# Reading the moving operand of a matmul as pairs of columns from its two halves

## The chip, the core and the metric

The kernel runs on one core of one Trainium2 chip. The metric is the device time of one launch in microseconds (us). The kernel before took 1817.81 us, the median of three runs (1817.16 to 1818.10).

## The reference

```python
x = A_x                                              # 1 x 2048 x 1024, float32
g = _sigmoid((x * gate_w).sum(-1, keepdims=True))
# A: Fourier mixing as dense matrices
a = jnp.einsum("bsd,ed->bse", x, dft_hid_re)
b = jnp.einsum("bsd,ed->bse", x, dft_hid_im)
y = jnp.einsum("ts,bse->bte", dft_seq_re, a) - jnp.einsum("ts,bse->bte", dft_seq_im, b)
# B: feed-forward, F = 3584
h = jnp.einsum("bsd,df->bsf", x, w1) + b1
r = jnp.where(h > 0, h, 0)
out = jnp.einsum("bsf,fd->bsd", r * r, w2) + b2
return g * y + (1 - g) * out
```

## The kernel before

**Stages.** Four matrix products follow one another. X multiplies `x` with the two hidden-dimension matrices (`w4`) and keeps the result `ab` in HBM. C multiplies the sequence matrices (`ct`) with `ab` and applies the gate. H multiplies `w1` with `x`, adds the bias, applies relu and square, and keeps `h` in HBM. O multiplies `w2` with `h`, adds the bias, applies `1 - g`, and adds C's part. By the loads of their inputs in the trace, C begins at about 241 us, H at about 810, O at about 1279.

**Fewer products, more sums.** Each stage is split into two by two blocks, and seven products replace eight (`FACTORS`); most of these are split into seven again (`twice`). VectorE makes the sums of blocks that this needs (tiles `sum`, `raw`, and the sums on results: `ab`, `y`, `h`, `o`, `u`).

**Three matmuls for one.** Every block is a tile of 128 partitions by 2 by 512 elements. An `Operand` splits it: ScalarE writes `hi`, the block rounded to the matmul's float32 type fp32r, and VectorE writes `lo`, what the rounding took away. `Group.run` (L542) then issues for each row block `r`, each half `kk` of the tile and each of the three pairs (hi·hi, hi·lo, lo·hi) one matmul. In all of them the stationary operand `st` is 128 columns wide, the moving operand `mv` is 512 columns wide, and the result fills 128 by 512 in PSUM (tile `ps`). These are the wide matmuls. The only others are 44 matmuls of 128 columns in bf16 on a tile `ones`, at the start (`WARM`).

**Who sets the order.** Nothing runs as it is written. The functions record operations; `plan` (L1372) then goes through a model of the machine and hands out each engine's order, the order of the DMA queues, and which of 55 SBUF slots each tile gets, by due times counted back from the matmuls. The model's time for one wide matmul is the constant `MM` (L39), in microseconds; all due times scale with it. TensorE's own order is not planned: matmuls go as recorded. `emit` (L1524) writes everything out, so nearly every row of the profile has its line, L1542. SyncE issues most loads, GpSimd the stores, the loads that add into SBUF or HBM, and some loads that the plan puts there.

**Layouts.** `kernel` (L1559) lays the inputs out in numpy before the launch: `x4`, `w4`, `ct` and `w1a`/`w1b`/`w2` as tiles for the stages, `xn` for the gate; it turns the output back after it. Those steps are outside the device time.

Of the kernel before, what the change touches and what calls it, by code (L numbers as in the profile page):

```python
# [15 lines left out]
P = 128  # L16
S, D, F = 2048, 1024, 3584
# [18 lines left out]
MADE = {"T1": 2568, "T3": 11876}  # L36
TWICE_H = (1, 2, 5, 3, 4, 6, 7), (1, 2, 5, 3, 4, 6)

MM, MM_END, FIRST_MM = 0.2267, 0.18, 6.2  # L39
VEC, VEC_END, ACT, ACT_END = (0.07, 1.0417e-3), 0.39, (0.09, 0.843e-3, 0.04, 0.095), 0.41  # L40
ADDING = 0.85, 2.1, 2.2
ISSUE, RING, RATE, SEM, LANES = {"sync": 0.36, "scalar": 0.36, "gpsimd": 0.56}, {"sync": (1.8, 1.8), "scalar": (1.8, 1.8), "gpsimd": (1.6, 1.6)}, (420e3, 395e3), 0.06, 8
# [33 lines left out]
def gated_mix_kernel(ctx: ExitStack, tc: tile.TileContext, x4, xn, w4, ct, w1a, w1b, w2, b1, b2, gw, out):  # L76
# [143 lines left out]
    def run(*parts):  # L220

        for _ in zip_longest(*parts):
            pass
# [57 lines left out]
    class Part(Near):  # L281
# [21 lines left out]
        def load(self, engines):  # L303
            if self.lands:
                self.slots = [take("raw", width=self.width)]
                a, b = (b.at if isinstance(b, Kept) else b for b in self.blocks)
                at = self.slots[0][:, :, 0:self.width]
                next(engines).dma_start(at, a)
                nc.gpsimd.dma_start(at, b, accum_op=ADD)
            else:  # L310
                run(self.load_parts(engines))
# [24 lines left out]
        def sum(self):  # L336
            run(self.make_parts())
# [59 lines left out]
    class Operand:  # L397
# [28 lines left out]
        def sum(self):  # L426
            run(self.sum_parts())
# [86 lines left out]
    class Group:  # L514
# [27 lines left out]
        def run(self, st, mv, by_part=False):  # L542
            if not self.ps:
                self.prepare()
            self.at += 1
            ends = self.at % self.k == 0
            mms = [(r, kk, n) for r in range(self.rows) for kk in range(2) for n in range(3)]
            if by_part:
                mms.sort(key=lambda e: (e[1], e[0] // 2, e[2], e[0]) if e[1] == 0 else (e[1], e[2], e[0]))
            for r, kk, n in mms:  # L550
                a, b = ((st.hi, mv.hi), (st.hi, mv.lo), (st.lo, mv.hi))[n]
                nc.tensor.matmul(self.ps[r // self.per][:, r % self.per, :], a[:, kk, r * P:(r + 1) * P],
                                 b[:, kk, :], start=self.at == 1 and kk + n == 0 and not self.onto,
                                 stop=ends and kk == 1 and n == 2,
                                 skip_group_check=bool(self.at > self.k or self.onto))
                if ends and self.per == 1 and kk == 1 and n == 2:
                    self.done[0][0](r // 2, self.ps[r], r % 2)
                elif ends and (r % 2 or r == self.rows - 1) and kk == 1 and n == 2:
                    self.done[self.at // self.k - 1][0](r // 2, self.ps[r // 2])
            if self.at == self.k * len(self.done):  # L560
                banks.extend(self.pools)
# [1031 lines left out]
```

## Time and profile before

| | |
|---|---|
| median of three runs | 1817.81 us |
| profiled execution, first to last instruction (its span) | 1816.2 us |
| outside the span, against the median | 1.6 us |
| TensorE busy | 1799.8 us, 99% |
| VectorE busy | 1711.6 us, 94% |
| ScalarE busy | 1157.5 us, 64% |
| GpSimd busy | 284.2 us, 16% |
| moved by DMA | 562.63 MB, 310 GB/s |
| mean granted TensorE clock | 0.999 |

The profile gives the span of its execution alone; the time outside it is taken from the runs. [...] And TensorE's weight load (PEld) lies beside the matmul before it.

### The profile page before, as it was taken

The page shows a single profiled execution, that of the slowest core. Times are in us where ns is not written, and L with a number is a line of the kernel's source. Part 1 is how long each engine was busy: PE and PEld are TensorE (multiplying, and loading weights), DVE is VectorE, ACT ScalarE, POOL GpSimd, SP SyncE. Part 2 cuts the span into 40 slices and gives each one's busy share as a digit, 9 for nine tenths or more (in the row PEclk, how much of TensorE's full clock was granted, in tenths as well). Part 3 has the DMA queues.
Part 4 walks back from the last instruction along what each step waited for, and adds up shares of the span by engine and source line. Part 5 has one row for each costly group of instructions (what it writes and reads, how often), then busy time and mean ns, then how long its engine had stood idle before and what let it go on. Part 6 is the DMA issues. An engine that isn't in the chain of part 4 may idle for free. (4 is left out here: it accounts for less than half of the span.)

```text
span 1816.2 us, 22349 instructions
## 1 busy us (share of the span) xinstructions
PE 1799.8 (99%) x7940; PEld 1484.5 (82%) x7940; DVE 1711.6 (94%) x1698; ACT 1157.5 (64%) x1274; POOL 284.2 (16%) x415
## 2 busy tenths in 40 slices
PE   9999999999999999999999999999999999999998
PEld 7888878888888888888878888788888888888886
DVE  8999989999999999999779999878998999999997
ACT  6465655774666664666583739967886567575662
POOL 1212112111211100111120201111121021101121
PEclk9999999999999999999999999999999999999999
DMA  9999999999998899989998889999999999979986
GB/s 376 322 393 380 384 331 302 323 273 292 261 354 264 227 306 383 311 216 351 314 371 278 279 299 329 375 381 327 345 362 253 335 241 303 328 192 349 316 218 149
DMA packets 158607, 562.63 MB, mean 310 GB/s; under 512 B 17808, under 2 KB 18080, under 8 KB 158496
## 3 DMA queue, kind: packets, MB, share of 16 engines
q1 hardware_dynamic: 98496, 351.99, 51.4%
q0 software_dynamic: 59712, 208.83, 43.1%
q8 instruction: 62, 1.02, 0.2%
q10 hardware_dynamic: 288, 0.39, 0.1%
q14 instruction: 49, 0.40, 0.1%
HBM read 402.28 MB, written 138.94 MB: 298 GB/s over the span
## 5 line engine op out<-in xcount | busy, mean ns | idle before, releaser
L1542 PE MATMUL ps<-hi 128*128 128x512 f32 x2188 | 852.2, 390 | 6.2 <-DVE h L1542 3.2
L1542 PE MATMUL ps<-hi,lo 128*128 128x512 f32 x2188 | 850.7, 389 | 1.0 <-DVE lo L1542 1.0
L1542 PE MATMUL ps<-lo,hi 128*128 128x512 f32 x2188 | 850.8, 389 | 0.6 <-DVE lo L1542 0.6
L1542 ACT ACTIVATE hi<-raw 128x1024 fp32r<-128x1024 f32 (+2 forms) x452 | 459.1, 1035 | 238.7 <-DVE raw L1542 76.1
L1542 PEld LDWEIGHTS ps<-hi 128*128 128x128 f32 x2188 | 410.6, 188 | 96.9 <-DVE h L1542 5.3
L1542 PEld LDWEIGHTS ps<-hi,lo 128*128 128x128 f32 x2188 | 410.7, 188 | 87.4 <-DVE lo L1542 1.8
L1542 PEld LDWEIGHTS ps<-lo,hi 128*128 128x128 f32 x2188 | 410.5, 188 | 86.4 <-DVE lo L1542 1.5
L1542 DVE TENSOR_TENSOR lo<-raw,hi 128x1024 fp32r<-128x1024 f32 (+2 forms) x385 | 451.5, 1190 | 29.1 <-ACT hi L1542 24.1
L1542 ACT ACTIVATE hi<-sum 128x1024 fp32r<-128x1024 f32 (+1 forms) x248 | 253.8, 1037 | 153.0 <-DVE sum L1542 103.3
L1542 DVE TENSOR_TENSOR lo<-sum,hi 128x1024 fp32r<-128x1024 f32 (+1 forms) x232 | 273.9, 1194 | 14.4 <-ACT hi L1542 5.4
L1542 PE MATMUL ps<-hi,both 128*128 128x512 f32 x888 | 285.0, 389 | 0.0
L1542 DVE TENSOR_TENSOR raw<-raw 128x1024 f32<-128x1024 f32 (+1 forms) x173 | 204.0, 1196 | 5.3 <-DMA raw<-in_w1a 2.6
L1542 PEld LDWEIGHTS ps<-hi,both 128*128 128x128 f32 x888 | 166.6, 188 | 34.7 <-DVE both L1542 0.2
L1542 DVE TENSOR_TENSOR sum<-raw 128x1024 f32<-128x1024 f32 (+2 forms) x180 | 175.6, 985 | 11.1 <-DMA raw<-in_w1a 2.3
L1542 PE MATMUL ps<-lo,both 128*128 128x512 f32 x444 | 172.7, 389 | 0.0
L1542 DVE TENSOR_TENSOR sum<-raw,sum 128x1024 f32<-128x1024 f32 (+2 forms) x135 | 141.3, 1049 | 2.3 <-DMA raw<-in_ct 1.4
L1542 ACT ACTIVATE u<-ps 128x1024 f32<-128x1024 f32 x104 | 101.2, 976 | 34.7 <-PE ps L1542 32.5
L1542 PEld LDWEIGHTS ps<-lo,both 128*128 128x128 f32 x444 | 83.4, 188 | 17.4
L1542 ACT ACTIVATE ps<-u 128x1024 f32<-128x1024 f32 x68 | 67.2, 989 | 35.5 <-DVE u L1542 16.3
L1542 DVE TENSOR_TENSOR u<-u,ps 128x1024 f32<-128x1024 f32 x74 | 86.8, 1184 | 1.9 <-PE ps L1542 1.0
L1542 ACT ACTIVATE both<-sum 128x512 fp32r<-128x512 f32 x74 | 46.3, 625 | 55.5 <-DVE sum L1542 49.2
L1542 DVE TENSOR_TENSOR h<-h,ps 128x1024 f32<-128x1024 f32 (+1 forms) x58 | 61.2, 1067 | 11.6 <-PE ps L1542 11.2
(82 smaller groups left out, 1002.2 us busy)
## 6 DMA issues: line engine op xcount, KB each, us to landing
raw<-in_ct SPq DMA_DIRECT2D x133, 512.0 KB, 8.9
raw<-h SPq DMA_DIRECT2D x104, 512.0 KB, 7.2
raw<-in_w SPq DMA_DIRECT2D x94, 512.0 KB, 9.0
raw<-copy SPq DMA_DIRECT2D x74, 512.0 KB, 7.1
raw<-ab SPq DMA_DIRECT2D x70, 512.0 KB, 10.0
raw<-in_x SPq DMA_DIRECT2D x51, 512.0 KB, 8.7
lo<-lo SPq DMA_DIRECT2D x50, 512.0 KB, 7.0
copy<-raw POOLq DMA_DIRECT2D x46, 512.0 KB, 9.3
```

What stands on the lines that cost most here:

```text
L1542: made = getattr(real[op.engine], op.name)(*(actual(a) for a in op.args), **{k: actual(v) for k, v in op.kwargs.items()})
```

## The change

One access pattern, one constant, and four layouts.

```diff
-MM, MM_END, FIRST_MM = 0.2267, 0.18, 6.2
+MM, MM_END, FIRST_MM = 0.2157, 0.18, 6.2
...
                 nc.tensor.matmul(self.ps[r // self.per][:, r % self.per, :], a[:, kk, r * P:(r + 1) * P],
-                                 b[:, kk, :], start=self.at == 1 and kk + n == 0 and not self.onto,
+                                 b[:, kk, :].rearrange("p (a b) -> p b a", a=2), start=self.at == 1 and kk + n == 0 and not self.onto,
...
+    seen = np.arange(512).reshape(2, 256).T.ravel()
+    twice = (512 * np.arange(4)[:, None] + seen[seen]).ravel()
...
-        "xn": x.reshape(P, 16, D).transpose(1, 0, 2),
-        "w4": np.stack([... for a in w]),
-        "ct": np.stack([... for a in c], axis=2),
+        "xn": x[twice].reshape(P, 16, D).transpose(1, 0, 2),
+        "w4": np.stack([... for a in w])[..., np.argsort(seen)],
+        "ct": np.stack([... for a in c], axis=2)[..., seen],
...
-    return np.ascontiguousarray(r.results[0]["out"].T).reshape(1, S, D)
+    return np.ascontiguousarray(r.results[0]["out"][:, np.argsort(twice)].T).reshape(1, S, D)
```

A wide matmul read the columns of its moving operand as 0, 1, 2, ... 511. Now it reads 0, 256, 1, 257, ... 255, 511: the pattern's inner dimension has two elements, 1024 bytes apart, and the outer one 256. The tile in SBUF, the stationary operand and the write to PSUM are as before. The columns of a result therefore stand in another order than those of its moving operand, and numpy's layouts make up for it: X's moving operand is stored the other way round, so `ab` is in plain order; H's result is in the order `seen`; O reads that in pairs again, so its columns are in `seen[seen]`, and `ct`, the gate's rows and the output follow. All of that is numpy's, before and after the launch; shapes and sizes of all transfers stay.

The constant changes the plan. Each engine still has the same instructions, by operation, names and shape, and the same number of DMAs on each queue; TensorE's row of matmuls is the same, and the orders of the four others change almost everywhere. Two places:

VectorE at the start of stage X, within its first twenty instructions; `sum` makes a sum of two blocks, `lo` a low part that a matmul waits for:

```order
-L1542 TENSOR_TENSOR lo<-sum,hi 128x1024
-L1542 TENSOR_TENSOR sum<-raw,sum 128x1024
-L1542 TENSOR_TENSOR lo<-raw,hi 128x1024
-L1542 TENSOR_TENSOR sum<-raw,sum 128x1024
-L1542 TENSOR_TENSOR lo<-sum,hi 128x1024
+L1542 TENSOR_TENSOR sum<-raw,sum 128x1024
+L1542 TENSOR_TENSOR lo<-sum,hi 128x1024
+L1542 TENSOR_TENSOR lo<-raw,hi 128x1024
+L1542 TENSOR_TENSOR lo<-sum,hi 128x1024
+L1542 TENSOR_TENSOR sum<-raw,sum 128x1024
```

One sum is made a place earlier and another a place later; the low parts between them keep their sequence.

ScalarE in the same stretch; `hi<-raw` and `hi<-sum` are the rounded parts of a block and of a sum, `u<-ps` empties a PSUM tile:

```order
 L1542 ACTIVATE hi<-raw 128x1024
 L1542 ACTIVATE u<-ps 128x1024
-L1542 ACTIVATE hi<-raw 128x1024
-L1542 ACTIVATE hi<-sum 128x1024
+L1542 ACTIVATE hi<-sum 128x1024
+L1542 ACTIVATE hi<-raw 128x1024
 L1542 ACTIVATE u<-ps 128x1024
 L1542 ACTIVATE hi<-sum 128x1024
```

Two rounded parts change places between two emptyings of PSUM.

More of the change, by code (lines that the diff above doesn't have):

```diff
@@ L1571 @@
              for j in range(2) for b in (16 + 6 * j,)]
+    seen = np.arange(512).reshape(2, 256).T.ravel()
+    twice = (512 * np.arange(4)[:, None] + seen[seen]).ravel()
     laid = {
         "x4": x.T.reshape(2, 2, 2, P, 4, 512).transpose(4, 0, 1, 3, 2, 5),
-        "xn": x.reshape(P, 16, D).transpose(1, 0, 2),
-        "w4": np.stack([a.T.reshape(2, 2, 2, P, 2, 512).transpose(4, 0, 1, 3, 2, 5) for a in w]),
-        "ct": np.stack([a.T.reshape(8, 2, P, 2, 2, 512).transpose(3, 4, 0, 2, 1, 5) for a in c], axis=2),
+        "xn": x[twice].reshape(P, 16, D).transpose(1, 0, 2),
+        "w4": np.stack([a.T.reshape(2, 2, 2, P, 2, 512).transpose(4, 0, 1, 3, 2, 5) for a in w])[..., np.argsort(seen)],
+        "ct": np.stack([a.T.reshape(8, 2, P, 2, 2, 512).transpose(3, 4, 0, 2, 1, 5) for a in c], axis=2)[..., seen],
         "w1a": w1[..., :2048].reshape(2, 2, 2, P, 2, 2, 512).transpose(4, 5, 0, 1, 3, 2, 6),
```

## The prediction

> **What bounds the kernel now.** I read the page's first part, then its chain and costliest groups, then the waits of TensorE, then the table by stage. The page's span and busy times, its chain, and the five groups of wide matmuls:
>
> ```profile
> span 1816.2 us, 22349 instructions
> PE 1799.8 (99%) x7940; PEld 1484.5 (82%) x7940; DVE 1711.6 (94%) x1698; ACT 1157.5 (64%) x1274; POOL 284.2 (16%) x415
> ...
> PE 27%; DVE 0%; issue 0%
> ...
> L1542 PE MATMUL ps<-hi 128*128 128x512 f32 x2188 | 852.2, 390 | 6.2 <-DVE h L1542 3.2
> L1542 PE MATMUL ps<-hi,lo 128*128 128x512 f32 x2188 | 850.7, 389 | 1.0 <-DVE lo L1542 1.0
> L1542 PE MATMUL ps<-lo,hi 128*128 128x512 f32 x2188 | 850.8, 389 | 0.6 <-DVE lo L1542 0.6
> ...
> L1542 PE MATMUL ps<-hi,both 128*128 128x512 f32 x888 | 285.0, 389 | 0.0
> ...
> L1542 PE MATMUL ps<-lo,both 128*128 128x512 f32 x444 | 172.7, 389 | 0.0
> ```
>
> 3 × 2188 + 888 + 444 = 7896 wide matmuls, and TensorE is idle before them for under 8 us in all. TensorE is the bound, by its own pace. The chain that ended last gives the pace over the last 491 us without a stop, and the start of the trace has what the 128-column bf16 matmuls do:
>
> ```profile
> 1314.76 491.29 PE ps L1542 x2166
> ```
>
> ```profile
> 1.06 4.42 PE L1542 MATMUL ps<-ones 128*128 128x128 bf16 x44 [1.06 <-DVE ones L1542]
> ```
>
> ```profile
> 4.87 0.61 PE L1542 MATMUL ps<-ones 128*128 128x128 bf16 x8
> ```
>
> ```profile
> L1542 PEld LDWEIGHTS <-ones x44: 97/147/147, 1.1 to 5.2; 128*128 128x128 bf16 x44
> L1542 PE MATMUL ps<-ones x44: 219/311/311, 1.1 to 5.3; 128*128 128x128 bf16 x44
> ```
>
> ```profile
> L1542 PEld LDWEIGHTS ps<-hi x2188: 186/188/189, 5.8 to 1807.7; 128*128 128x128 f32 x199
> ```
>
> Wide matmuls start every 491.29 / 2166 = 226.8 ns. Of the 44 small ones 36 start between 1.06 and 4.87 us, 105.8 ns apart; the last eight cover 0.61 us, the last of them itself 0.219, so they start (0.61 − 0.219) / 7 = 55.9 ns apart. I read the step as TensorE's clock doubling: 105.8 halved is 52.9 ns for 128 columns, and 3.0 ns are left over for each matmul. Four times 52.9 is 211.6 ns for 512 columns, 214.6 with one such rest. So a wide matmul takes about 12 ns more than the small ones let expect, everywhere, beside a busy or an idle VectorE: it is something each wide matmul does itself. The weight load is an unlikely cause: on `ones` it lasts at least 97 ns and is hidden under a pace of 55.9, and on `hi` its 188 ns are 39 less than the pace. What is left is the streaming of 512 columns of four bytes, and 12 in 212 is about one lost step in eighteen columns.
>
> The table by stage says what comes next when TensorE speeds up: columns are length, then busy time and instructions of TensorE, its weight load, VectorE, ScalarE and GpSimd, then clock, DMA share, GB/s.
>
> ```profile
> 0.00:10.00 10.00, 8.60 (x61) 7.41 (x62) 3.56 (x7) 5.24 (x8) 0.20 (x4) 1.00 0.79 272
> 10.00:100.00 90.00, 89.00 (x391) 72.54 (x390) 89.64 (x80) 52.52 (x53) 20.32 (x35) 1.00 1.00 364
> 100.00:200.00 100.00, 99.88 (x441) 82.40 (x440) 99.81 (x105) 57.22 (x59) 18.04 (x34) 1.00 1.00 390
> 200.00:400.00 200.00, 198.04 (x872) 163.11 (x871) 187.89 (x188) 128.06 (x139) 37.18 (x54) 1.00 0.98 313
> 400.00:600.00 200.00, 200.00 (x884) 165.62 (x883) 195.64 (x190) 118.13 (x126) 34.74 (x47) 1.00 0.96 296
> 600.00:800.00 200.00, 200.00 (x884) 165.62 (x883) 195.70 (x194) 119.91 (x129) 23.36 (x28) 1.00 0.95 299
> 800.00:1000.00 200.00, 197.62 (x869) 162.44 (x868) 175.72 (x157) 125.47 (x134) 26.96 (x44) 1.00 0.91 313
> 1000.00:1200.00 200.00, 198.61 (x874) 163.47 (x873) 185.24 (x184) 155.68 (x191) 24.93 (x42) 1.00 0.92 326
> 1200.00:1400.00 200.00, 199.31 (x876) 163.80 (x875) 178.60 (x198) 148.56 (x181) 38.15 (x59) 1.00 1.00 335
> 1400.00:1600.00 200.00, 200.00 (x884) 165.60 (x883) 199.08 (x200) 126.45 (x135) 31.08 (x40) 1.00 0.97 292
> 1600.00:1800.00 200.00, 200.00 (x884) 165.58 (x884) 192.53 (x194) 119.68 (x128) 26.13 (x27) 1.00 0.88 257
> 1800.00:1817.00 17.00, 8.75 (x39) 6.93 (x37) 8.24 (x11) 0.60 (x1) 3.14 (x3) 0.91 0.60 123
> ```
>
> VectorE has no room from 10 to 200 us and from 1400 to 1600, little from 400 to 800, and 15 to 24 us in each 200 from 800 to 1400.
>
> **The change part by part.** *The read in pairs.* No row shows a moving operand read in another order, so its price is bounded. At best every wide matmul falls to 214.6 ns, 12.2 less; if the 3.0 ns of a small matmul go with its columns, four times 55.9 is 223.6, 3.2 less. On the other side each column may cost a second step, 2 × 211.6 = 423 ns, or 196 more. The nearest rows for an engine that takes columns from two places in turn are VectorE's:
>
> ```profile
> L1542 DVE TENSOR_TENSOR lo<-raw,hi 128x1024 fp32r<-128x1024 f32 x354 | 424.4, 1217 | 15.8 <-ACT hi L1542 12.4 <-PE ps L1542 1.8 <-DMA copy<-raw 0.6
> ...
> L1542 DVE TENSOR_TENSOR ab<-ab,ps 128x1024 f32<-128x1024 f32 x32 | 38.6, 1210 | 0.0
> ```
>
> Two operands in SBUF (`raw`, `hi`) take 1217 ns, one in SBUF and one in PSUM 1210: reading two places of SBUF column by column costs it nothing to speak of. [...] I take 11.0 ns less, the difference of the two constants in the diff, near the good end; a loss this small and regular looks like a hiccup of a run along neighbouring columns, which two runs taken in turn would hide. TensorE alone then gains 7896 × 11.0 = 86.9 us.
>
> [...]
>
> *What is late next.* With TensorE faster, each stage lasts as long as the longer of two: its length less 0.011 us for each of its matmuls, or its VectorE busy time. In order of the table, with both ends kept: 10 + 89.6 + 99.8 + 190.4 + 195.6 + 195.7 + 190.4 + 190.4 + 190.4 + 199.1 + 192.5 + 17 = 1760.9, and 0.8 less since the last row runs past the span: 1760.1. So 56.1 us of the 86.9 arrive; VectorE takes back the other 30.8. VectorE can be as full as that: it is 99.8 of 100 us from 100 to 200. With the 1.6 us outside the span, 1761.7. I add 2.3 us for places within a stage where VectorE is late and has no earlier work to lend (TensorE's waits, mostly on VectorE, are a few us now) and take 1764.
>
> *The new plan.* Same instructions, same bytes; VectorE's two swapped rows and ScalarE's cost nothing in themselves. If the pace comes as planned, the due times fit the machine better. If they move wrongly, the price is like the waits of now:
>
> ```profile
> PE ps L1542 <- DVE h L1542: 3.2, 4, 1.4
> PE ps L1542 <- DVE lo L1542: 1.6, 2, 1.0
> PE ps L1542 <- DVE ab L1542: 1.3, 1, 1.3
> PE ps L1542 <- DVE u L1542: 1.1, 2, 0.9
> ```
>
> These four come to 7.2 us; doubled or gone, the new order is worth −7 to +7. On SyncE's queue loads change places by one or two, on GpSimd's stores and loads do too; what waits behind a GpSimd issue is a store, and nothing of TensorE waits for those now. Layouts in numpy: nothing, the transfers keep shape and size.
>
> *DMA.* Its queues are the other thing near the end of its room:
>
> ```profile
> q1 hardware_dynamic: 98496, 351.99, 51.4%
> q0 software_dynamic: 59712, 208.83, 43.1%
> ```
>
> Together 94.5% of the engines' span. If stages with a share of 0.97 and more cannot shrink, 200 to 400, 1200 to 1400 and 1400 to 1600 keep their 200 us: 9.6 + 9.6 + 0.9 = 20 more, 1784 in place of 1764. If instead VectorE's work can all be moved between stages, TensorE sets the end: 1816.2 − 86.9 + 1.6 = 1731, which leaves VectorE 18 us idle in all. I keep both as ends.
>
> **The rivals.** *The pace stays.* If the extra is paid per instruction for the four-byte type, or by the swap of four-byte weights, the order of columns is nothing to it. For it: no row has wide matmuls of another width, so a part per matmul and a part per column can't be told apart. Against it: 12 ns are four times the rest of a small matmul. The new plan alone then moves the time by the ±7 above: 1811 to 1825, likeliest 1818.
>
> *Pairs cost.* This is the side on which I would be wrong in sign. If leaving a run of neighbouring columns is what costs, the plain order leaves one rarely and the pairs leave one at every column. With a second step for each column, 1816.2 + 7896 × 0.196 + 1.6 = 3365 us; with one for every other column, half of that, 2592. It decides early: each ns of pace is 7.9 us, so half a ns above 226.8 is already slower. For it: 12 in 212 fits a loss of one step at the end of a run. Against it: VectorE's two rows, and that the loss would then have to be as large per run as a whole step and the run not even a power of two (212 / 12 = 17.7, though a ns of rounding gives 16).
>
> [...]
>
> *A part only.* At 223.6 ns the gain is 7896 × 3.2 = 25 us, under what VectorE has free in every stage but 10 to 200 and 1400 to 1600: 1793 to 1798.
>
> **How the numbers follow.** Pace down to about 215.7 and VectorE next: 0.66, 1731 to 1784, likeliest 1764. A part only: 0.08, around 1795. Pace stays: 0.12, of which faster 0.02, the same 0.08, slower 0.02. Pairs cost: 0.14, far above. Differences under 0.2% (3.6 us, from 1814.2 to 1821.4) are about what a measurement can't tell from no change. Faster is 0.66 + 0.08 + 0.02 = 0.76, same 0.08, slower 0.02 + 0.14 = 0.16. The range runs from 1735, since the lowest end needs VectorE free to lend everything, up to 1821: that takes in the part and the unchanged pace, and leaves out the pairs that cost.
>
> **What would show it.** Right: starts of wide matmuls about 215.7 ns apart in a stretch without waits; VectorE's busy time still near 1712 us, but 97% of the span; TensorE waiting 30 us or more on VectorE's `lo`, `sum`, `ab` and `o` in 10 to 200, 400 to 800 and 1400 to 1600, and nearly none from 800 to 1400. Wrong: a pace of 226.8 with an unchanged table (the extra is the instruction's own), a pace above it (the pairs cost), or waits of TensorE on DMA landings (the queues were the next bound).

## The result, and the profile after

The changed kernel takes 1800.74 us (median of four runs, 1799.66 to 1801.71), the one before 1817.49 beside it: a ratio of 0.9908, interval 0.9894 to 0.9922. It is 16.8 us faster where the prediction had 54. The profiled execution has a span of 1797.9 us.

The page of the changed kernel: span, busy times, chain, and the three large groups of wide matmuls.

```profile
span 1797.9 us, 22340 instructions
PE 1737.2 (97%) x7940; PEld 1503.5 (84%) x7940; DVE 1707.9 (95%) x1698; ACT 1149.0 (64%) x1274; POOL 284.4 (16%) x415
...
PE 21%; DVE 6%; DMA 5%; issue 4%; ACT 1%; POOL 1%; POOLq 0%; DVEq 0%; SPq 0%; ACTq 0%
...
L1542 PE MATMUL ps<-lo,hi 128*128 128x512 f32 x2188 | 833.3, 381 | 17.7 <-DMA lo<-raw 12.6
L1542 PE MATMUL ps<-hi 128*128 128x512 f32 x2188 | 834.5, 382 | 12.1 <-ACT hi L1542 5.9
L1542 PE MATMUL ps<-hi,lo 128*128 128x512 f32 x2188 | 833.8, 381 | 9.8 <-DVE lo L1542 9.7
```

The chain that ended last was one unbroken piece of TensorE from 1315 us on; now it passes through VectorE, loads and GpSimd. The idle time ahead of these three groups was 7.8 us and is 39.6.

TensorE's row by time, in a stretch without waits, and after the longest wait:

```profile
1464.77 0.38 PE L1542 MATMUL ps<-lo,hi 128*128 128x512 f32 x1
...
1466.06 0.38 PE L1542 MATMUL ps<-lo,hi 128*128 128x512 f32 x1
...
1665.39 0.64 PE L1542 MATMUL ps<-hi,lo 128*128 128x512 f32 x1
1665.82 0.64 PE L1542 MATMUL ps<-hi 128*128 128x512 f32 x1
```

A matmul's row lasts 0.38 us and the next starts 0.215 us after it, so matmuls overlap, and what counts is the distance between two starts, the pace. Six distances in 1.29 us are 215 ns each (215.8 on average over all undisturbed ones): the pace is what the constant in the diff said, 215.7. At 1665 us the distance is 430 ns, about twice that: TensorE runs at half clock there, for 5.3 us after a wait (the granted clock is 0.56 from 1664 to 1671 us). In this trace 60 matmuls do; in the one before, none.

TensorE's waits in the changed kernel, the four largest sums (us in total, times, longest):

```profile
PE ps L1542 <- DVE lo L1542: 14.1, 14, 1.9
PE ps L1542 <- DMA lo<-raw: 12.6, 1, 12.6
PE ps L1542 <- DMA lo<-sum: 6.9, 4, 3.1
PE ps L1542 <- ACT hi L1542: 5.9, 4, 2.8
```

All of TensorE's waits come to 51.7 us: 19.2 on VectorE, 19.5 on loads that add onto a low part, 13.0 on ScalarE.

By start times the sum closes. From the first wide matmul to the last, the pace saves 86.8 us. The distances over the pace, half clock aside, grow by 53.5, from 12.7 to 66.2 us; half clock adds 12.7 (60 × 0.211), and the small remainder of the pace (215.8 for 215.7) adds 1.0: 86.8 − 53.5 − 12.7 − 1.0 = 19.6 us, the difference of the two traces by start times (18.3 in the spans).

The table by stage, with the columns of the table before, cut where the same matmuls stand as at 10, 100, 200, 400, ... 1800 us before:

```profile
10.20:102.20 92.00, 87.05 (x390) 74.27 (x390) 91.68 (x82) 51.82 (x53) 20.19 (x35) 0.98 1.00 368
102.20:199.70 97.50, 95.60 (x440) 82.72 (x440) 96.60 (x102) 55.73 (x58) 18.07 (x34) 1.00 0.99 380
199.70:395.80 196.10, 191.33 (x872) 166.21 (x872) 185.82 (x186) 126.34 (x137) 37.20 (x54) 0.98 1.00 320
395.80:593.70 197.90, 194.96 (x884) 168.61 (x883) 194.03 (x189) 117.71 (x126) 31.90 (x44) 0.98 0.96 295
593.70:793.70 200.00, 193.62 (x884) 167.51 (x882) 197.47 (x197) 119.27 (x129) 26.36 (x32) 0.99 0.96 306
793.70:984.50 190.80, 188.36 (x869) 163.47 (x868) 175.86 (x158) 126.15 (x135) 26.82 (x43) 1.00 0.93 328
984.50:1176.20 191.70, 189.66 (x875) 164.69 (x874) 183.08 (x183) 151.11 (x186) 24.17 (x41) 1.00 0.94 331
1176.20:1368.20 192.00, 189.69 (x876) 165.02 (x875) 172.34 (x192) 146.31 (x181) 36.34 (x56) 1.00 1.00 343
1368.20:1570.40 202.20, 195.47 (x884) 168.60 (x883) 199.24 (x198) 127.59 (x138) 33.16 (x42) 0.98 0.98 301
1570.40:1781.30 210.90, 195.14 (x885) 168.28 (x884) 199.84 (x202) 120.90 (x130) 26.88 (x28) 0.97 0.85 246
```

Where VectorE had room, from 794 to 1368 us, the 600 us of before take 574.5, near the forecast (571.2). That is partly the luck of this order: in the six other orders with the pairs, which follow below, the same matmuls take 580.6 to 598.7 us. Where VectorE had no room the stages take their VectorE time or more, and from 1570 on the changed kernel is slower than before by 10.9 us for the same matmuls.

### The profile page after: what moved, and what is told of

It reads as the page before. It is cut to its first block, busy times and chain, and to the rows that moved or that the text cites. A ratio compares the mean times of both kernels' runs of the same rounds, so it can differ in the third digit from the quotient of the medians.

```text
span 1797.9 us, 22340 instructions
## 1 busy us (share of the span) xinstructions
PE 1737.2 (97%) x7940; PEld 1503.5 (84%) x7940; DVE 1707.9 (95%) x1698; ACT 1149.0 (64%) x1274; POOL 284.4 (16%) x415
## 5 line engine op out<-in xcount | busy, mean ns | idle before, releaser
L1542 PE MATMUL ps<-lo,hi 128*128 128x512 f32 x2188 | 833.3, 381 | 17.7 <-DMA lo<-raw 12.6
L1542 PE MATMUL ps<-hi 128*128 128x512 f32 x2188 | 834.5, 382 | 12.1 <-ACT hi L1542 5.9
L1542 PE MATMUL ps<-hi,lo 128*128 128x512 f32 x2188 | 833.8, 381 | 9.8 <-DVE lo L1542 9.7
L1542 PEld LDWEIGHTS ps<-lo,hi 128*128 128x128 f32 x2188 | 416.0, 190 | 78.8 <-DMA lo<-raw 13.0
L1542 PEld LDWEIGHTS ps<-hi 128*128 128x128 f32 x2188 | 416.2, 190 | 78.6 <-ACT hi L1542 7.2
L1542 PEld LDWEIGHTS ps<-hi,lo 128*128 128x128 f32 x2188 | 415.9, 190 | 73.5 <-DVE lo L1542 14.7
L1542 PE MATMUL ps<-hi,both 128*128 128x512 f32 x888 | 281.4, 385 | 5.2 <-ACT both L1542 2.9
L1542 ACT ACTIVATE both<-sum 128x512 fp32r<-128x512 f32 x74 | 46.2, 625 | 66.4 <-DVE sum L1542 66.2
L1542 ACT ACTIVATE ps<-u 128x1024 f32<-128x1024 f32 x68 | 66.9, 985 | 26.2 <-DVE u L1542 13.0
```

Of the source, the lines that this page charges most:

```text
L1542: made = getattr(real[op.engine], op.name)(*(actual(a) for a in op.args), **{k: actual(v) for k, v in op.kwargs.items()})
```

## The experiments

For all of them one number serves, the **rest**: the span less 7896 times the pace (226.7 ns plain, 215.7 in pairs). It holds the start, the end, every wait and the half clock. Before, it is 1816.2 − 1790.0 = 26.2 us; in the changed kernel 1797.9 − 1703.2 = 94.7.

**The read alone, and the order alone.** First the pairs with the old constant:

```diff
-MM, MM_END, FIRST_MM = 0.2157, 0.18, 6.2
+MM, MM_END, FIRST_MM = 0.2267, 0.18, 6.2
```

> The read in pairs with the plan's constant back at 0.2267, so every engine has the order of the kernel before. Theory A (the read gives 11 ns per matmul, and VectorE's stages take most of it back whatever the order): pace 215.7 ns, time 1795 to 1812 us, TensorE idle 50 us or more. Rival B (the new order is bad, the old one would have let the gain through): near 1765 us. Rival C (the gain came from the new order): near 1817 us.

1808.52 us, ratio 0.9950 (0.9937 to 0.9962), the pace 215.8, rest 103.5. The time is in theory A's range: the read alone, in the old order, gives 8 us. Theory A's reason is not the whole of it. From 800 to 1400 us, where VectorE had room, the same matmuls take 598.7 us, almost as long as with the plain read, and none of TensorE's waits is on an adding load; the largest is on ScalarE, which writes sums back into PSUM:

```profile
PE ps L1542 <- ACT ps L1542: 27.0, 18, 3.3
```

Then the plain read with the new constant (before, with the first line of the diff alone):

> The plain read with the plan's constant at 0.2157, so every engine has the order of the changed kernel. Theory A: pace 226.7 ns as before and 1815 to 1825 us, since TensorE is again the bound and the order is made for a faster one. Rival C (the gain is the order's): near 1801 us with a pace of 226.7. Rival B (the new order is bad by itself): above 1825 us.

1856.74 us, ratio 1.0216 (1.0202 to 1.0230), the pace 226.7, rest 62.5. Theory A's range is missed and only rival B's "above 1825" holds: under the old pace the new order by itself costs 40 us. But B's other half failed in the run above: the old order did not let the gain through (near 1765 us, where 1808.52 was measured). TensorE's two largest sums of waits here:

```profile
PE ps L1542 <- DMA lo<-raw: 11.1, 1, 11.1
PE ps L1542 <- DVE lo L1542: 10.1, 11, 1.9
```

The wait of 11 us is the same one as the 12.6 us in the changed kernel, at the same place in GpSimd's row. GpSimd's row by time in the changed kernel:

```profile
1634.43 2.43 POOL L1542 DMA_DIRECT2D out<-o  x2 [0.95 <-DVE o L1542]
1642.05 1.19 POOL L1542 DMA_DIRECT2D out<-o  x1 [5.18 <-DVE raw L1542]
1645.97 0.90 POOL L1542 DMA_DIRECT2D lo<-raw  x1 [2.73 <-issue]
```

And the same place in the plain read with the new order:

```profile
1684.98 1.20 POOL L1542 DMA_DIRECT2D out<-o  x1 [1.35 <-DVE o L1542]
1686.72 1.21 POOL L1542 DMA_DIRECT2D out<-o  x1 [0.54 <-DVE o L1542]
1692.62 1.19 POOL L1542 DMA_DIRECT2D out<-o  x1 [4.69 <-DVE raw L1542]
1696.43 0.90 POOL L1542 DMA_DIRECT2D lo<-raw  x1 [2.62 <-ACT hi L1542]
```

A load that adds a block onto its low part (`lo<-raw`) stands behind four stores that add to the output (with one load among them, in either run) and wait mostly for VectorE. That belongs to the order, since it is there at both paces. Being issued late is not the whole of this wait, though. The chain shows the load itself:

```profile
1645.97 18.79 DMA lo<-raw
```

It takes 18.79 us to land (18.81 in the other run); the median of the 22 such loads in this trace is 8.8 us. TensorE began to wait at about 1652.2 us, so with the median the wait would have been under 3 us in place of 12.6, by this estimate. The share of the DMA engines was 1.06 meanwhile (from 1651 to 1664 us), and the four stores ahead of it took 11 to 20 us to land. No run parts the late issue from the slow landing.

**VectorE relieved.** Every fourth low part is written by ScalarE, as a copy of the block; the kernel leaves out its subtraction:

```diff
-                nc.vector.tensor_tensor(self.lo[:, k, c], self.block.slot[:, k, c],
-                                        self.hi[:, k, c].bitcast(F32), op=SUB)
+                if lows[0] % 4 == 0:
+                    nc.scalar.activation(self.lo[:, k, c], self.block.slot[:, k, c], AF.Copy)
+                else:
...
```

> The changed kernel, in which every fourth low part is written by ScalarE as a plain copy of the block and not by VectorE as a difference. It leaves out that subtraction; VectorE loses some 180 instructions of 1.14 us, about 200 of its 1708 us, and ScalarE gains about as much on its 1149. Theory A (VectorE is what takes the gain back): VectorE far from full, TensorE's waits down from 52 us to 10 to 20, no stretches at half clock, 1725 to 1745 us. Rival D (loads and the GpSimd queue set the waits): 1785 us or more, TensorE still idle 40 us or more.

1769.35 us, ratio 0.9743 (0.9728 to 0.9758); VectorE 1532 us busy, rest 62.0. It is 31 us faster, and short of theory A's range by 24; rival D's is missed as well. TensorE's waits fall to 33 us and not to 10 to 20: a wait of 8 us on an adding load, with half clock behind it, is among what stayed.

**The adding loads left out.** The low parts that ScalarE begins are left unfinished:

```diff
-                nc.gpsimd.dma_start(self.lo.bitcast(F32), self.block.slot, accum_op=ADD)
```

> The changed kernel without the loads by which GpSimd adds a block onto its negated rounded part (the low parts that ScalarE begins and a DMA ends); it leaves out that addition. VectorE keeps its work; GpSimd's queue loses those issues, and the DMA engines their bytes. Theory A (VectorE first; the adding loads only pass its lateness on, because they stand behind stores that wait for VectorE): TensorE's waits on these loads, 19.5 us, and the half clock behind the longest of them go, but waits on VectorE stay, 1775 to 1790 us. Rival D (GpSimd's queue and the DMA are the next bound): 1755 to 1770 us.

1780.74 us, ratio 0.9799 (0.9786 to 0.9813), rest 76.6, in theory A's range; TensorE's waits on VectorE's `lo` stay (17.8 us).

**Other orders.** The plan's constant at 0.2187, 0.2217 and 0.2172:

> The changed kernel with the plan's constant at 0.2187 instead of 0.2157: another order of the same instructions. Theory A as it stands now (VectorE is next, and an order made for a pace that VectorE cannot follow adds waits by its place in GpSimd's and ScalarE's queues): pace 215.7, fewer waits than with 0.2157, 1780 to 1798 us. Rival F (the order is a matter of chance, every constant gives another sum of waits): anywhere from 1785 to 1815 us. Rival G (the order is without effect): 1801 us.

1793.35 us, ratio 0.9868 (0.9853 to 0.9883), rest 88.6: in theory A's range, and in F's; G is out.

> The changed kernel with the plan's constant at 0.2217, the mean time for one matmul in a kernel of 1760 us. Theory A as it stands now: an order for the pace that VectorE permits, 1770 to 1790 us, below the run at 0.2187. Rival F (chance): 1785 to 1815 us and no slope from 0.2157 over 0.2187 and 0.2217 to 0.2267 (1801 and 1809 at the ends). Rival G: 1801 us.

1799.36 us, ratio 0.9904 (0.9889 to 0.9919), rest 93.7: above theory A's range and above the run at 0.2187; within F's range.

> The changed kernel with the plan's constant at 0.2172, between 0.2157 (1801 us) and 0.2187 (1793). If the order's quality follows the constant, about 1797 us. Rival F (chance): anything from 1785 to 1810 us, away from that line by more than 4 us.

1794.58 us, ratio 0.9871 (0.9851 to 0.9891), rest 89.8. It lies 2.4 us off the line's 1797, so it is nearer to the line than rival F asked for.

And two orders in which the plan takes GpSimd's DMAs to land later:

```diff
-"gpsimd": (1.6, 1.6)}
+"gpsimd": (1.6, 6.0)}
```

> The changed kernel with one more constant of the plan: a DMA issued by GpSimd is taken to land 4.4 us later than before (6.0 for 1.6), so that the plan issues those loads and stores earlier. Theory H (part of the loss is the order's own: loads that add stand behind stores on GpSimd's queue and land in 18.8 us at the longest wait): TensorE's waits on these loads, 19.5 us, go to under 6, the half clock behind them too, 1770 to 1788 us. Theory A alone (they pass on VectorE's lateness, which no order removes): 1795 to 1805 us, other waits take their place.

1794.33 us, ratio 0.9872 (0.9857 to 0.9887), rest 89.1. TensorE's waits on adding loads fall from 19.5 to 0.7 us, as theory H had it; its waits on others rise:

```profile
PE ps L1542 <- DVE lo L1542: 15.2, 18, 2.0
PE ps L1542 <- ACT ps L1542: 10.1, 7, 4.1
```

Of the 19.5 us only 6 arrive in the time, which is 6 us above theory H's range and just under the one of theory A alone.

> The same with the plan's constant at 0.2187. Theory H: below the 1793 us of 0.2187 without it, by the 4.2 us of waits on adding loads that were left there and some half clock: 1782 to 1790 us. Rival F (every constant gives its own order, and the sum of waits is chance): between 1785 and 1810 us.

1801.12 us, ratio 0.9910 (0.9895 to 0.9924), rest 97.3. Theory H's range is missed and rival F's holds: two edits that help one by one don't add up.

So seven orders of the same work end between 1793 and 1809 us. Over the constant alone, from 0.2157 to 0.2267, the five times are 1800.7, 1794.6, 1793.4, 1799.4 and 1808.5 us: a shallow valley, which five runs can't tell from chance. The fastest version that leaves nothing out is the changed kernel with 0.2187; it differs from the run at 0.2172 and from the first of the two later-landing orders by less than their intervals.

**Both reliefs.** ScalarE's copies, and no adding loads:

> The two reliefs in one kernel: every fourth low part copied by ScalarE (VectorE's subtraction left out there), and the loads that add a block onto its negated rounded part left out. Theory A (VectorE is the next bound, the adding loads behind GpSimd's stores the one after it): TensorE's waits under 20 us, 1730 to 1750 us. Rival D' (ordinary loads are late, since the DMA engines have no room): 1755 us or more, and TensorE's waits lead back to landings of raw tiles.

1742.59 us, ratio 0.9592 (0.9576 to 0.9608), rest 37.4, where theory A had it. Its chain ends in one piece of TensorE again:

```profile
1323.04 404.33 PE ps L1547 x1871
```

404.33 / 1871 = 216.1 ns.

**VectorE alone.** What was left of the cause was told apart by leaving out one in three full-width low parts of VectorE, so that ScalarE and GpSimd keep their work (the matmuls read the high part in place of it, and the results lack those low parts):

```diff
+            if self.width > 256 and not self.keep:
+                lows[0] += 1
+                if lows[0] % 3 == 0:
+                    self.lo = self.hi
+                    self.block.used()
+                    return
```

> The changed kernel in which one in three of the full-width low parts that VectorE makes (192 of its 728 low parts) is left out; the matmuls that would read it read the high part instead, so TensorE, ScalarE and the loads that add keep their work, and the results lack those low parts. It relieves VectorE alone. Theory A (VectorE is the next bound; what stayed in the run with copies on ScalarE came from ScalarE and the adding loads): waits plus half clock at 20 to 35 us, 1735 to 1755 us. Rival D (loads that add and GpSimd's queue keep their own 20 us or more whatever VectorE does): 1760 us or more, with waits on the adding loads of 10 us or more.

1756.05 us, ratio 0.9663 (0.9649 to 0.9677), rest 49.7. Its busy times, from the page:

```profile
PE 1722.2 (98%) x7940; PEld 1498.3 (85%) x7940; DVE 1506.4 (86%) x1506; ACT 1150.7 (66%) x1274; POOL 284.6 (16%) x415
```

And the one wait of TensorE on an adding load that is left:

```profile
PE ps L1550 <- DMA lo<-sum: 2.1, 1, 2.1
```

With VectorE at 86% the adding loads all but cease to be late, though GpSimd has as many. The time is 1 us beyond theory A's range, and short of rival D's. All these kernels with work left out also get a new order from the plan; the gain of 45 us here is more than the 15 us by which the seven orders differ.

**Less room ahead.** 51 SBUF slots for 55:

> The changed kernel with 51 SBUF slots in place of 55, so that less can be made ahead. Theory A in its plain form (VectorE's stages take their busy time, whatever is ahead): 1796 to 1808 us. Rival I (what limits is how far ahead VectorE, ScalarE and the loads can get, since slots are full): 1815 us or more, with longer stages from 200 to 400 and from 1600 on.

1831.38 us, ratio 1.0079 (1.0062 to 1.0096), rest 126.3: 31 us more than with 55, as rival I had it for the time. It had the place wrong. By the same matmuls as above, the stretch from 200 to 400 us gets shorter (189.6 for 196.1) and the last one grows by 3 us; 22 of the 31 us are in the 574.5 of 800 to 1400 us, where VectorE had room, and 13 between 400 and 800. So room ahead matters, but the run doesn't show that it is VectorE's crowded stages that need it.

**Orders of columns, by themselves.** Sections of matmuls with nothing beside them. Each row is a section: start, length, tile, count; the distance to the next row's start over the count is the mean pace.

> Matmuls alone, in sections of 64 (128 and 256 for the two narrow ones), on one tile of fp32r and one of bf16, with no other engine at work: it computes none of the reference. Sections: bf16 to warm up, then fp32r with columns in plain order, in pairs from the two halves, in fours from quarters, sixteen from sixteenths, even columns then odd, every fourth column, runs of 4 and of 16 columns taken in turn from the two halves, pairs 4 columns apart, plain at 256 and at 128 columns wide, bf16 plain and in pairs, and plain and pairs once more. Theory A (the plain read of four-byte columns loses one step in sixteen columns, two places in turn hide it): plain 226.7, pairs 215.7, plain at 256 and 128 columns 113 to 115 and 57 (the loss goes with the columns), bf16 215.7 both ways. Rival E (a fixed rest per fp32r matmul that the pairs remove): plain at 128 columns 67 (53.3 and 13.3). [...]

```profile
37.05 13.98 PE L25 MATMUL pairs<-mv,st 128*128 128x512 f32 x64
50.86 18.28 PE L25 MATMUL fours<-mv,st 128*128 128x512 f32 x64
68.98 28.01 PE L25 MATMUL sixteens<-mv,st 128*128 128x512 f32 x64
96.79 29.06 PE L25 MATMUL evenodd<-mv,st 128*128 128x512 f32 x64
125.67 29.70 PE L25 MATMUL stepfour<-mv,st 128*128 128x512 f32 x64
155.20 16.19 PE L25 MATMUL blockfour<-mv,st 128*128 128x512 f32 x64
171.22 15.53 PE L25 MATMUL blocksixteen<-mv,st 128*128 128x512 f32 x64
186.59 13.98 PE L25 MATMUL nearpairs<-mv,st 128*128 128x512 f32 x64
200.41 15.51 PE L25 MATMUL halfwidth<-mv,st 128*128 128x256 f32 x128
215.75 28.70 PE L25 MATMUL quarterwidth<-mv,st 128*128 128x128 f32 x256
...
258.12 31.16 PE L25 MATMUL bfpairs<-mb,sbf 128*128 128x512 bf16 x64
288.67 15.14 PE L25 MATMUL again<-mv,st 128*128 128x512 f32 x64
```

Pairs 215.8 ns, fours 283, sixteens 435, even then odd 451, every fourth column 461, pairs 4 columns apart 215.9; plain settles at 226.7 once the first few have passed. Runs of 4 and of 16 columns taken in turn from the two halves take 250 and 240, more than plain, so of the orders in this run only single columns taken in turn from two places help. bf16 in pairs settles at 484 (477 with the first ones), more than twice its plain 215.8, where theory A had no difference. At 256 columns plain fp32r settles at 120.0: rival E, not theory A. At 128 it takes 111.5, more than either had; what binds there is not shown.

> Matmuls alone again, no part of the reference. Plain fp32r at 512, 448 and 384 columns; pairs from the two halves at 384 and 256; pairs at 512 with 2, 8 and 64 columns between the two; bf16 in pairs 4 columns apart, bf16 plain at 512 and 256. Theory A (one step lost in sixteen columns): plain 198.3 ns at 448 and 170.0 at 384. Rival E (a fixed rest of 13.3 ns per plain fp32r matmul, which the section 256 wide, 120.0 ns, already favoured): 200.0 and 173.3. Pairs at 384: 162.4 ns (a rest of 2.4). Pairs of any distance: 215.7, as with 4 and 256.

```profile
36.64 11.28 PE L25 MATMUL plainthreequarters<-mv,st 128*128 128x384 f32 x64
47.76 13.38 PE L25 MATMUL plainseveneighths<-mv,st 128*128 128x448 f32 x64
60.98 10.56 PE L25 MATMUL pairsthreequarters<-mv,st 128*128 128x384 f32 x64
71.38 14.45 PE L25 MATMUL pairshalf<-mv,st 128*128 128x256 f32 x128
85.67 14.72 PE L25 MATMUL apartbytwo<-mv,st 128*128 128x512 f32 x64
100.22 13.98 PE L25 MATMUL apartbyeight<-mv,st 128*128 128x512 f32 x64
114.04 13.98 PE L25 MATMUL apartbysixtyfour<-mv,st 128*128 128x512 f32 x64
```

Plain at 384 settles at 173.3 (E: 173.3; A: 170.0). Pairs at 384 take 162.5, so 128 columns more cost 53.3 ns (215.8 − 162.5); at that price per column, plain fp32r pays about 13.3 ns over its columns at 256, 384 and 512 alike. At 448 it takes 206.7, about 20 over its columns, which neither had. Pairs at 256 take 111.6, the same as plain at 128. Pairs 8 and 64 columns apart take 215.8; 2 apart they take 227, as plain, where the expectation had 215.7 for any distance.

## Why the prediction was wrong

**The pace: right in size, not in its reason.** 10.9 ns less (226.7 to 215.8), 86 us on TensorE, none of the rivals *pace stays*, *pairs cost* or *a part only*. The 11.0 was taken from the two constants in the diff and not derived. The reason given, a loss in proportion to the columns, is not the right one: the extra is about 13.3 ns at 256, 384 and 512 columns alike, and the hit is luck to that extent. The step at the start that the prediction read as the clock doubling stands in the trace of the kernel before: starts fall from 107 to 56 ns apart where the first clock record begins, at full clock, at 4.85 us. The 52.9 ns for 128 columns that it took from there are near the 53.3 that 128 columns more cost in pairs. The rival *pairs cost* fails for fp32r in pairs: at 512 columns no order measured is faster than their 215.8 ns. A cost as large as that rival's shows in other orders: 484 ns for bf16 in pairs, 451 for fp32r with even columns then odd; fours take 283.

**The next bound: right in name, in part.** VectorE relieved alone takes the rest from 94.7 to 49.7 us. But TensorE waits on VectorE itself for 19.2 us, not for the 30 or more that was to show it; and one of the prediction's signs of being wrong did appear, 19.5 us of waits on DMA landings. With the adding loads left out the rest falls by 18 us, and with both reliefs by 57.

**The term that failed: 2.3 us for lateness within stages.** The prediction took each stage's floor, the longer of TensorE's and VectorE's time, and added almost nothing. By the floors 56.1 us were to arrive and 18.3 did in the spans, so the term should have been 37.8 us. What filled it were TensorE's waits and the half clock behind them. The stages came out as follows, in us; the last column is the shortest that any of the seven orders with the pairs reached.

| stretch before | forecast | after | VectorE busy after | best of seven orders |
|---|---|---|---|---|
| 10–100 | 89.6 | 92.0 | 91.7 | 89.9 |
| 100–200 | 99.8 | 97.5 | 96.6 | 97.3 |
| 200–400 | 190.4 | 196.1 | 185.8 | 192.3 |
| 400–600 | 195.6 | 197.9 | 194.0 | 194.4 |
| 600–800 | 195.7 | 200.0 | 197.5 | 196.4 |
| 800–1400 | 571.2 | 574.5 | 531.3 | 574.5 |
| 1400–1600 | 199.1 | 202.2 | 199.2 | 196.2 |
| 1600–1800 | 192.5 | 210.9 | 199.8 | 199.8 |
| sum | 1733.9 | 1771.1 | 1696.0 | 1740.8 |

The sum of the floors was sized well: picked stretch by stretch from seven orders, the shortest come within 7 us of it, though the last stretch stays 7.3 us above its floor in all of them and three others go under theirs. No one order reaches them all, and that is what the term should have paid for. 37 us are missing in this table. Half of it, 18.4, is the last stretch: VectorE had 199.8 us of work there and not 192.5, and the late adding load cost TensorE 12.6 us more, with half clock after it. That VectorE could make less in advance because the stage ahead of it was full fits this, and no run singles it out.

The floors also left out ScalarE, which in the changed kernel is busy for 99.9 of the 102 us from 1074 to 1176.

**The new plan: mis-sized.** It was priced at −7 to +7. Under the old pace the new order costs 40 us, under the new pace it gains 8: the order's worth was not to be read from the waits of before, and the prediction's reading of GpSimd's queue ("nothing of TensorE waits for those now") named the wrong cargo; the loads that add stand in that queue too.

**A cost not thought of: the clock.** TensorE waits long enough to fall to half clock, 12.7 us in all. By the clock records of the changed kernel's trace, these stretches start on a fixed grid of 3.41 us and last one step of it or several (3.41 to 13.65 us). In the traces of the kernels before and after, TensorE's rows leave it idle for under 1.5 us in 1029 steps at full clock, and half clock follows none of them; it follows all seven steps with 2.0 us or more, and two of the six between. So a step need not be idle throughout: in the changed kernel, 1.85 us from 94.3 us on were enough, and 1.71 us from 804.4 us on were not. All five of its waits of over 2 us met half clock, also the two that fall across two steps (3.14 us as 0.63 and 2.51, 2.90 us as 0.41 and 2.49).

**DMA as the next bound** (1784 us in the prediction): not by room on the engines. With VectorE relieved the same bytes go through in 1753 us. A single load was late all the same: the 18.79 us above fell where their share was 1.06, and no run shows whether that made it slow.

**What stays open.** Leaving low parts out also frees their slots, and fewer slots cost 31 us, so how much of those 45 us is VectorE's busy time and how much the room ahead is not told apart. The run with ScalarE's copies bears on it, since every low part keeps its slot there: the rest still falls by 33 us; but those copies need not wait for the high part either. Open too is why the old order with the pairs gains almost nothing from 800 to 1400 us, where VectorE had room. So is why plain fp32r matmuls pay 13.3 ns, and 20 at 448 columns.

## What to carry to other kernels

When one engine at 99% is made faster beside another at 94%, take the stage-by-stage maximum as the floor and not as the forecast: here 87 us of gain met a floor at 56, and a real order reached 17, the best of seven 24. Price what stands in a queue behind the engine that becomes the bound, and how long it takes to land there. For fp32r matmuls of 512 columns, reading single columns from two places in turn (4, 8, 64 and 256 columns apart were measured) is worth 11 ns each (226.7 to 215.8). bf16 should stay plain: pairs from the two halves took 484 ns there for 215.8.

## What the runs showed of the hardware that was not expected

A moving operand in plain order is not the fastest: at 512 columns of fp32r, pairs take 215.8 ns, plain 226.7, fours 283, every fourth column 461. With bf16 the same pairs from the two halves take 484 and plain 215.8, while pairs 4 columns apart take 216. And half clock followed all seven 3.41 us steps of a fixed grid in which TensorE idled for 2.0 us or more in the traces of the kernels before and after: once the wait of 12.6 us was over, eleven distances of 427 ns cost 2.3 us more.
